# Holding raw stores and the rounding of seven late weight blocks until the first layer is nearly done

## The chip, the cores and the metric

One core of one Trainium2 chip runs the whole program. The metric is the device time of one execution in microseconds (us), the median of several runs. Other names used throughout: TensorE (PE in the profile) does the matrix products, ScalarE (ACT), VectorE (DVE) and GpSimd (POOL) the elementwise work, SyncE (SP) issues most DMA transfers. Lines of the changed kernel stand seven lines lower than the same lines of the kernel before from line 290 on (L872 there is L879 here, L881 is L888, L349 is L356).

## The reference, cut to what matters

```python
# attention, 8 batches, 8 heads, 576 tokens, 64 per head
q_s = exp(q - max(q, -1));  q_s = q_s / (sum(q_s, -1) + 1e-9)       # per token and head
k_s = exp(k - max(k, 2));   k_s = k_s / (sum(k_s, 2) + 1e-9)        # over the tokens
x = einsum(q_s, einsum(k_s, v))                                     # then (batch, token, 512)
# Fourier mixing and a feed-forward block
u  = x + real(fft(fft(x, axis=1), axis=2))
un = (u - mean(u)) / sqrt(var(u) + 1e-6)
out = u + maximum(un @ w_ch1, 0) @ w_ch2        # w_ch1 512 x 2048, w_ch2 2048 x 512
```

The two weights arrive as 64-bit floats. The kernel reads them as pairs of 32-bit words and rounds them to 32-bit floats on the chip.

## The kernel before

Group 0 (the first batch) uses the weights while they are still arriving. They come in 32 blocks of 512 KB, 0 to 15 of the first weight, 16 to 31 of the second. TensorE runs the first layer of group 0 as 16 products ("f"), then its second layer (the "down stage"). The attention and the Fourier mixing of batch 1 are woven into the down stage, and the same stage computes combinations of weight quarters, which are stored to HBM so that later groups can use a multiplication with seven products instead of eight. From the next group on nothing of this recurs.

Rounding a block takes two passes on ScalarE, two on VectorE, and one addition on GpSimd. The intermediate `t` lies in PSUM for blocks below 20, and over the block's own raw words, in SBUF, for the rest.

```python
n = ("bc", "bb", "bc", "bb")[i] if i < 4 else "acc"
if i < 20:
    t = self.ps.tile([P, 512], F32, tag=n, name=n, bufs=3 if i >= 4 else 1)[:]   # PSUM
else:
    t = hi.bitcast(F32)                                                          # SBUF
...
nc.scalar.activation(t, hi.bitcast(F32), ACT.Copy, scale=2.0 ** -112)                      # L347
V.tensor_scalar(out=to, in0=ti, scalar1=3, ..., op0=ALU.logical_shift_left)                # L348
V.scalar_tensor_tensor(out=to, in0=ti, scalar=-(1 << 31), in1=to, ...)                     # L349
nc.scalar.activation(lo, lo.bitcast(U32), ACT.Copy, scale=2.0 ** -29)                      # L352
nc.gpsimd.tensor_tensor(out=out, in0=to, in1=lo, op=ALU.add)                               # L353
```

Raw words wait in places that are used again. After a block is rounded, the next block of the same place is fetched:

```python
def round_blocks(some):
    for i in some:
        convert(i)
        if i in after:
            fetch(after[i])          # 29 takes the place of 25, 31 that of 26
...
for f in range(NF):                  # the first layer, one product and one Relu each
    up[f]()
    free(f)                          # at f 12 queries may be loaded, at 15 keys and values, quarters stored
    round_blocks(...)
rest = [lambda i=i: round_blocks([i]) for i in range(4 + n, 2 * NF)]   # 20 to 31, woven into the down stage
...
# in combine(layer, p), which stores combinations
if layer and p % 4 == 3:
    four = self.spare_words          # pairs 3 and 7: in "spare", the same memory as unT
```

The program gives each engine its order by a static schedule made at build time, so a block that stands "in the down stage" of the program may be rounded during the layer, as soon as its words are there. `unT` is the normalized, turned input of a group's first layer.

## Time and profile before

The time is 1136.21 us (3 runs, 1135.63 to 1138.32). What matters is read off TensorE's timeline, from the first product of the layer to the first product of the next group (L942). "End gap" is from the end of the last down matmul (its start in the timeline plus 0.43 us for each record) to that product, so it holds the last turns of the input too.

| stage, kernel before | us |
|---|---|
| first layer, first product to first down matmul | 66.48 (with one wait of 7.41) |
| down stage | 73.45 (with waits of 0.60 and 1.15) |
| end gap | 1.28 |
| start of the next group | 204.44 |

Two stretches of the windows view, the beginning of the down stage. The columns are the stretch, its length, then busy time (and instruction count) of TensorE, its weight loads, VectorE, ScalarE and GpSimd, TensorE's granted clock, the DMA share and GB/s:

```profile
117.20:129.70 12.50, 12.49 (x24) 5.44 (x25) 4.53 (x11) 7.48 (x23) 3.39 (x4) 0.83 0.33 109
129.70:146.00 16.30, 15.70 (x49) 7.64 (x48) 13.59 (x33) 8.20 (x24) 9.94 (x12) 1.00 0.88 321
```

### The profile page before, as it was taken

The numbers are of one execution on the slowest core, as the hardware profiler recorded it, in microseconds if no ns is written. First come the engines' busy times: TensorE is split into PE (matmuls) and PEld (weight loads), VectorE is DVE, ScalarE is ACT, GpSimd is POOL, SyncE is SP. The second block draws the span as 40 slices with busy tenths as digits, with TensorE's granted clock in tenths as the row PEclk, the third lists the DMA queues.
The fourth block names the chain that finished last, engine by engine and source line by source line (L and its number), as shares of the span: only waits on it lengthen the run. The fifth ranks groups of instructions, "written<-read, shape, count | busy, mean of one in ns | idle before, by whom it ended". The sixth has DMA issues, their size and how long they took to land.

```text
span 1134.4 us, 14587 instructions
## 1 busy us (share of the span) xinstructions
PE 1094.5 (96%) x5440; PEld 915.5 (81%) x5440; DVE 542.3 (48%) x1109; ACT 404.3 (36%) x975; POOL 335.3 (30%) x304
## 2 busy tenths in 40 slices
PE   5798899999999999999999999999999999999997
PEld 4643355888888988898889888888889888888886
DVE  6776586368433734375344733583434352203201
ACT  6694423355333513362325322442334152201200
POOL 2065382226103510334023402261034203302320
PEclk9999899999999999999999999999999999999999
DMA  9556668354346534544356335552453344434441
GB/s 304 174 200 186 231 218 303 116 206 176 111 151 220 185 142 145 194 157 176 127 176 220 149 102 179 193 200 107 144 193 148 116 156 156 182 143 156 151 186 55
DMA packets 92581, 193.79 MB, mean 171 GB/s; under 512 B 23120, under 2 KB 59728, under 8 KB 85344
## 3 DMA queue, kind: packets, MB, share of 16 engines
q1 hardware_dynamic: 90712, 191.82, 49.2%
q10 hardware_dynamic: 1800, 1.05, 0.3%
q8 instruction: 43, 0.70, 0.2%
q14 instruction: 26, 0.21, 0.1%
HBM read 168.72 MB, written 28.31 MB: 174 GB/s over the span
## 4 chain that ended last, share of the span: by engine, by line
PE 86%; ACT 4%; DMA 3%; DVE 3%; issue 2%; POOL 1%; ACTq 0%; SPq 0%; POOLq 0%; DVEq 0%
PE bb L942 15%; PE bb L980 15%; PE ba L942 10%; PE bc L980 10%; PE bc L942 10%; PE ba L980 10%; PE acc L563 3%; PE acc L645 2%; PE acc L738 2%; PE acc L741 2%; PE acc L762 2%; PE tr L613 1%; PE tr L842 1%; PE bc L881 1%; PE tr L549 1%
## 5 line engine op out<-in xcount | busy, mean ns | idle before, releaser
L942 PE MATMUL bb<-unT,big 128*128 128x256 f32 x768 | 187.4, 381 | 0.0
L980 PE MATMUL bb<-big 128*128 128x256 f32 x768 | 172.1, 379 | 0.0
L942 PEld LDWEIGHTS bb<-unT,big 128*128 128x128 f32 x768 | 142.8, 190 | 23.6 <-DVE u L910 2.6
L980 PEld LDWEIGHTS bb<-big 128*128 128x128 f32 x768 | 145.4, 190 | 20.3
L359 POOL TENSOR_TENSOR big<-big 128x512 f32<-128x512 f32 (+1 forms) x38 | 46.2, 1217 | 305.9 <-ACT big L954 305.9
L942 PE MATMUL bc<-unT,big 128*128 128x256 f32 x512 | 125.4, 379 | 0.0
L954 ACT ACTIVATE big<-big 128x512 f32<-128x512 f32 x96 | 60.3, 629 | 182.6 <-DVE big L953 182.1
L942 PE MATMUL ba<-unT,big 128*128 128x256 f32 x512 | 123.6, 379 | 0.2 <-ACT unT L846 0.2
L980 PE MATMUL bc<-big 128*128 128x256 f32 x512 | 116.0, 379 | 0.5 <-DVE x L997 0.5
L980 PE MATMUL ba<-big 128*128 128x256 f32 x512 | 114.8, 379 | 0.0
L914 DVE TENSOR_TENSOR u<-bb,s 128x512 f32<-128x512 f32 x40 | 27.6, 691 | 177.8 <-PE bb L980 120.4
L980 PEld LDWEIGHTS bc<-big 128*128 128x128 f32 x512 | 96.1, 190 | 14.3 <-DVE x L997 0.9
L980 PEld LDWEIGHTS ba<-big 128*128 128x128 f32 x512 | 95.7, 190 | 12.1
L942 PEld LDWEIGHTS bc<-unT,big 128*128 128x128 f32 x512 | 95.1, 190 | 12.6
L942 PEld LDWEIGHTS ba<-unT,big 128*128 128x128 f32 x512 | 95.1, 190 | 12.2 <-ACT unT L846 0.5
L367 POOL TENSOR_TENSOR unT<-unT 128x512 f32<-128x512 f32 x8 | 14.2, 1774 | 182.1 <-DVE unT L366 182.1
L602 ACT ACTIVATE q<-q,qm 128x64 f32<-128x64 f32 x240 | 61.6, 339 | 6.1 <-DVE qm L600 6.0
L910 DVE TENSOR_TENSOR u<-bb,s 128x512 f32<-128x512 f32 x40 | 27.6, 690 | 73.3 <-PE bb L942 38.7
L953 DVE TENSOR_TENSOR big<-bc,u 128x512 f32<-128x512 f32 x64 | 44.1, 689 | 22.8 <-PE bc L942 21.7
L992 POOL TENSOR_TENSOR x<-x,u 128x512 f32<-128x512 f32 x14 | 17.7, 1267 | 113.9 <-DVE u L914 101.3
L846 ACT COPY unT<-tr 128x512 f32<-128x512 f32 x36 | 20.7, 586 | 79.7 <-PE tr L842 79.1
L953 DVE TENSOR_TENSOR big<-bb,s 128x512 f32<-128x512 f32 x32 | 22.1, 690 | 55.6 <-PE bb L942 55.5
(248 smaller groups left out, 1653.9 us busy)
## 6 DMA issues: line engine op xcount, KB each, us to landing
big<-w1s SPq DMA_DIRECT2D x64, 896.0 KB
big<-w2s SPq DMA_DIRECT2D x56, 1024.0 KB
big<-in_w_dram SPq DMA_DIRECT2D x21, 512.0 KB
q<-in_q_dram SPq DMA_DIRECT2D x27, 256.0 KB
k<-in_kT_dram SPq DMA_DIRECT2D x24, 288.0 KB
v<-in_v_dram SPq DMA_DIRECT2D x24, 256.0 KB
words<-in_w_dram SPq DMA_DIRECT2D x8, 512.0 KB
mirror<-x SPq DMA_DIRECT2D x14, 256.0 KB
```

The costliest lines, as they stand in the source:

```text
L359: e1.tensor_tensor(out=to(4), in0=at(2), in1=at(3), op=ALU.add)
L563: nc.tensor.matmul(pk, lhsT=ks[:, c, :], rhs=v[:, c, :], start=(c == 0), stop=(c == NC - 1))
L602: nc.scalar.activation(heads[:, h, :], heads[:, h, :], ACT.Exp, bias=m[:, h:h + 1])
L645: nc.tensor.matmul(px[:, r * P:(r + 1) * P], lhsT=qT[:, r, :], rhs=self.kvr[b % 2][:, r, :], start=True, stop=True)
L738: nc.tensor.matmul(full[:, at:at + size], lhsT=t[:, own], rhs=self.ft[:, f + at:f + at + size], start=at == 0, stop=False, skip_group_chec ...
L741: nc.tensor.matmul(full[:, 0:NM], lhsT=g[:, tail], rhs=self.ft[:, f:f + NM], start=False, stop=True, skip_group_check=True)
L910: V.tensor_tensor(out=temp("u2"), in0=box["bb"][:], in1=box["s1"][:], op=ALU.add)
L914: V.tensor_tensor(out=temp("u3"), in0=box["bb"][:], in1=box["s1"][:], op=ALU.add)
L942: nc.tensor.matmul(bank()[:, i, :], lhsT=w[:, WA_AT[m], k * P:(k + 1) * P], rhs=unT[:, B_AT[m], k, :], start=first and i == 0 and k == 0, ...
L953: V.tensor_tensor(out=hp(i), in0=bank[:], in1=u[:], op=ALU.add)
L954: nc.scalar.activation(hp(i), hp(i), ACT.Relu)
L980: nc.tensor.matmul(bank()[:, i, :], lhsT=h[p][:, A_AT[m], i * P:(i + 1) * P], rhs=w[:, p, :], start=first and i == 0 and p == 0, stop=p == ...
```

## The change

Its intent is to get late roundings and the first weight's stores out of the way of the layer. A gate is a tiny VectorE instruction that reads one tile and rewrites a few words of another, so that users of the second wait for the first. Here blocks 20 to 26 wait for the Relu of product 13, and the raw quarters' stores wait for the end of the layer.

```diff
             for t in held.get(f, ()):
                 copy(t, self.h0[0:1, f, 0:1])
-            if f == NF - 1:
-                copy(self.w1sb[0:1, :, 0:1], self.w1sb[0:1, :, 0:1])
         return free
+
+    def hold_stores(self):
+        for w in (self.w1sb[0:1, :, ::HD], self.w2sb[0:1, 0:3, ::HD]):
+            self.nc.vector.tensor_copy(w, w)
+        for i in range(NF + 4, 2 * NF):
+            if i in self.raws:
+                self.gate(self.h0[:, NF - 3, :], self.raws[i][0:1, 0:2])
 ...
                 round_blocks(range(4 + n * f // NF, 4 + n * (f + 1) // NF))
+            blk.hold_stores()
             rest = ...
```

## The prediction

> **What bounds the kernel now.** I read the page first, then TensorE's timeline from 56 to 206 us, then the timelines of the other engines over the gaps found there. TensorE is busy 96% of the span, so a change is worth only what it does to TensorE's gaps (and to the clock after them). The change touches one place: the stage between the first feed-forward layer of batch 0 and the first layer of the next group. Compiled instruction orders of the two kernels, which need no chip, are the same on TensorE from end to end, and on every engine again from about 20 us into the next group. The other ~925 us can only be shifted.
>
> ```profile
> span 1134.4 us, 14587 instructions
> PE 1094.5 (96%) x5440; PEld 915.5 (81%) x5440; DVE 542.3 (48%) x1109; ACT 404.3 (36%) x975; POOL 335.3 (30%) x304
> ```
>
> TensorE's timeline (start, length, line, count of records, idle time before): the one large gap, and the end of the stage.
>
> ```profile
> 106.20 3.60 PE L872 MATMUL ba<-unT,big 128*128 128x512 f32 x8
> 117.21 5.80 PE L872 MATMUL bb<-unT,big 128*128 128x512 f32 x8 [7.41 <-ACT big L874]
> 122.84 3.60 PE L872 MATMUL bc<-unT,big 128*128 128x512 f32 x8
> 126.27 3.60 PE L872 MATMUL ba<-unT,big 128*128 128x512 f32 x8
> 129.71 3.60 PE L881 MATMUL bc<-big 128*128 128x512 f32 x8
> ...
> 202.30 1.02 PE L881 MATMUL bc<-big 128*128 128x512 f32 x2
> 203.16 1.04 PE L842 MATMUL tr<-ident,eo 128*128 128x128 f32 x8
> 204.44 1.99 PE L942 MATMUL ba<-unT,big 128*128 128x256 f32 x8 [0.24 <-ACT unT L846]
> ```
>
> Each f of the layer takes 3.43 us (start to start). Product 13 waits 7.41 us for a Relu that frees its bank, then takes 5.63 instead of 3.43. Why is that Relu late? ScalarE's timeline:
>
> ```profile
> 101.12 0.58 ACT L874 ACTIVATE big<-ba 128x512 f32<-128x512 f32 x1
> 111.53 0.65 ACT L347 ACTIVATE big<-big 128x512 f32<-128x512 f32 x1 [9.82 <-DMA big<-in_w_dram]
> 112.09 0.66 ACT L352 ACTIVATE big<-big 128x512 int32<-128x512 uint32 x1
> 115.38 0.65 ACT L347 ACTIVATE words<-words 128x512 f32<-128x512 f32 x1 [2.63 <-DMA words<-in_w_dram]
> 115.94 0.66 ACT L352 ACTIVATE words<-words 128x512 int32<-128x512 uint32 x1
> 116.49 0.57 ACT L874 ACTIVATE big<-bb 128x512 f32<-128x512 f32 x1
> ```
>
> ScalarE is not short of work time; it sits at the rounding of blocks 29 and 31, whose words were only requested at 107.98 and 110.04, and Relu 10 stands behind them. That is what the change removes. At the stage's end, unT (the normalized input of the next group) is copied from 201.25 on:
>
> ```profile
> 201.25 0.59 ACT L846 COPY unT<-tr 128x512 f32<-128x512 f32 x1
> 203.80 1.08 ACT L846 COPY unT<-tr 128x512 f32<-128x512 f32 x2 [0.71 <-PE tr L842]
> ```
>
> Its tile is the same memory as "spare", which holds raw words and, for combination pairs 3 and 7 of the second weight, four results. Before, that is over in time (GpSimd, then the queue issues the store):
>
> ```profile
> 184.60 0.73 POOL L369 TENSOR_TENSOR spare<-big,spare 128x256 f32<-128x256 f32 x1 [0.36 <-DVE spare L368]
> 189.63 1.10 SPq L402 DMA_DIRECT2D w2s<-spare x1
> ```
>
> **What the Trainium skill says.** "PSUM — Partial Sum Buffer", section "Engine vs sequencer instructions": the queues of ScalarE, VectorE and GpSimd are strict FIFO. The trace agrees: Relu 10 had its product by about 103 us and ran at 116.49, behind two roundings. "TensorE: Matmul & The Clock Gate", section "What's actually happening": after an idle window of about 3.4 us the array falls to half clock and needs about as long of busy time to come back. The trace agrees: 5.63 against 3.43 us after the gap, 2.2 us lost. "DMA: Bandwidth & Descriptors", section "Specifications": about 358 GB/s per core from HBM. From 157 to 195 us this trace moved 336 GB/s with the engines 98% busy, which I use, though single slices reached 423.
>
> **The change part by part.**
>
> *Layer one.* After the change the roundings of blocks 20 to 26 stand behind Relu 13 (a gate on VectorE reads Relu 13's output and each raw block), and the fetches of 29 and 31, which need the places of 25 and 26, come later still. Relu 8 to 13 stand directly behind one another. So product 13 starts at 106.20 + 3.43 = 109.63, 14 at 113.07, 15 at 116.50, and the down stage at 119.94 instead of 129.71: **-9.77 us** (7.41 wait, 2.2 clock, rest rounding).
>
> *What is moved into the down stage.* Seven blocks times ScalarE 2 x 0.56 = 7.8 us, VectorE 0.43 + 0.69 = 7.8 us, GpSimd 1.28 = 9.0 us; VectorE's gates cost 7 x 0.08 = 0.6. Stores: 8 of 128 KB (first weight's raw quarter), 2 of 128 and 5 of 256 KB (second weight), plus two fetches of 512 KB: 3.6 MB, at 336 GB/s 10.7 us of transfer, into a stretch whose DMA was 9% busy for 11 us (146 to 157). In bytes it fits, with nothing over.
> Call the start of the down stage D. TensorE's own order sets deadlines, read off the old timeline: first query turned at D+8.6, block 20 needed at D+10.7, query copies at D+14.3, +18.9, +22.9, +26.8, block 24 at D+25.9, block 28 at D+38.9. Walking the new orders with the durations above from q landing at about 113.4 (requested at 110.7 once Relu 12 is done, plus 2.8 as in the old trace): blocks 20 to 23 are rounded by about 126 (deadline 130.7), the first query is ready at about 126.7 (128.5), blocks 24 to 27 by 138 (145.8). The tight one is the third query copy, D+22.9 = 142.8: ahead of it on ScalarE stands block 29, fetched at about 136.5 and landing 4.2 to 5.2 us later (as 95.3 to 99.5 and 110.0 to 115.3 in the old trace), then 2 x 0.56 + two copies of 0.5: about 143.5. I allow **+1.0 us**. Against that, the old waits of 0.60 (query copy) and 1.15 us (Z copies behind two key exponentials; now one stands there, later) probably go: **-1.5 us**.
>
> *The end of the stage.* This I take to decide the case. In the new orders VectorE runs the second key's gate and maximum, and the combinations of pairs 6 and 7, **behind** the last down output (it waits for the last down matmul, old time 203.16). ScalarE's second key exponential stands before the unT copies, and the first unT copy also waits for the store w2s<-spare of pair 7. In old time, with durations from the old trace: output add 203.36 to 204.0, gate and key maximum to 204.8, exponential with its accumulator read to 205.7, reciprocal to 206.0, pair 6 on VectorE (2 x 0.43) to 206.9, pair 7 (0.43 + 0.83) to 208.2, GpSimd's last 0.73 to 209.4, store issued at 209.5 behind 0.9 MB of others, landed about 4 us later (a 512 KB store in the chain took 0.35 + 3.56) at 213.5. Then a copy 0.6, turn 0.64, copy 0.6, and the next group's first product at about 215.5 instead of 204.44: **+11.1 us**. TensorE is idle for 11 us there, so it starts cold: **+2.1 us**, the same as the old loss at 117 and 1.8 at 63.23 (5.37 against 3.60).
>
> Sum: -9.77 + 1.0 - 1.5 + 11.1 + 2.1 = +2.9 us; 1136.2 + 2.9 = 1139.1, and I take **1138.5 us** since the +1.0 may not come. The gap is moved from 110 us to the end of the down stage and hardly shrinks.
>
> **The rivals.**
> (a) The gain comes through: the unT copies do not really wait for the pair 7 store (I misread which transfer their semaphore stands for), only for the key exponential. Then the end costs 3.2 us (first copy at 205.7 instead of 201.25, third at 207.0) and perhaps 1 of clock, and the time is about 1130. For it: the gap of 7.4 us is real and goes. Against: the store reads the tile that the copy overwrites, so some wait must stand there.
> (b) The DMA queue or the in-order issue becomes the bound in the down stage: SyncE's queue issues in order, and behind a blocked store stand fetches 29 and 31 and the keys. For it: 98% busy DMA from 157 to 195 before, 3.6 MB more now. Against: 11 idle microseconds before it, and 9 idle after. It would add 3 to 6 us of waits at the query copies or at the Z copies: about 1143.
> (c) The shift is hidden: nothing, because later stages absorb it. Against: TensorE is over 99% busy from 204 on, with the same order, so a shift at 204 goes through to the end whole.
>
> **Range and chances.** (a) gives 1130, mine 1138.5, (b) 1143. I give mine two chances in three and the others most of the rest. Predicted **1138.5 us**, 8 in 10 between **1131.5** and **1144.0**. 2% is 22.7 us, which no rival reaches: faster 0.01, same 0.97, slower 0.02.
>
> **What would show it.** Right: no gap before product 13, its 8 records 3.6 us long; the down stage starts near 120; between the last L881 matmul and the first matmul of the next group about 11 us, ended by ScalarE's unT copy, and that copy waiting for DMA w2s<-spare; the next group's first matmuls slow; group start near 207 with the clock loss. Wrong: a first copy that waits only for the key exponential (rival a); TensorE waiting several microseconds on query or Z copies between 130 and 190 (rival b); stores landing much faster or slower than 4 us; pair 7 already combined before the last down matmul.

## The result, and the profile after

| | before | after |
|---|---|---|
| time, median (range, runs) | 1135.92 (1134.13 to 1138.32, 4) | 1151.45 (1148.95 to 1153.52, 4) |
| first layer | 66.48 | 56.70 |
| down stage | 73.45 | 87.87 |
| end gap | 1.28 | 12.61 |
| start of the next group | 204.44 | 218.93 |

The ratio is 1.0134, 95% interval 1.0106 to 1.0163. Ratios here and below are the mean time of one kernel's runs over that of the other's in the same rounds, so they are not quite the ratio of the medians. The change made the kernel 15 us slower; 1138.5 had been predicted, and the range ended at 1144.0.

TensorE's timeline of the changed kernel (start, length, line, record count, idle time before and its releaser):

```profile
108.15 3.60 PE L879 MATMUL bb<-unT,big 128*128 128x512 f32 x8
...
118.45 3.60 PE L888 MATMUL bc<-big 128*128 128x512 f32 x8
...
129.43 0.63 PE L620 MATMUL tr<-ident,q 128*128 128x128 f32 x4 [2.23 <-issue]
...
147.01 1.56 PE L652 MATMUL acc<-kvr,qT 128*128 128x128 f32 x8 [2.29 <-ACT qT L627]
...
174.74 0.73 PE L745 MATMUL acc<-ft,eo 128*128 128x144 f32 x4 [1.46 <-DVE eo L713]
187.42 0.71 PE L769 MATMUL acc<-cd,Z 128*128 128x128 f32 x4 [2.39 <-ACT Z L751]
...
217.14 1.97 PE L849 MATMUL tr<-ident,eo 128*128 128x128 f32 x8 [10.66 <-ACT unT L853]
```

Product 13 starts at 108.15 with no wait: the large gap of the layer is gone. The last line is the gap at the end that had been predicted. The four between were not: with one of 0.95 us at 149.52 they make 9.32 us of waits in the down stage, against 1.75 before. Three of them also cost clock: the work from 129.43 to 136.74 took 7.3 us and took 5.6 before, that of 147.01 to 155.0 took 7.0 (without the 0.95) against 3.9, that of 187.4 to 192.1 took 4.6 against 2.8, in sum 6.6 us. Waits and clock together account for the stage's 14.4 us.

The same two stretches as above, now of the changed kernel:

```profile
117.20:129.70 12.50, 10.27 (x27) 4.45 (x26) 11.81 (x20) 11.94 (x35) 11.14 (x11) 1.00 0.71 236
129.70:146.00 16.30, 15.02 (x52) 7.82 (x50) 16.30 (x26) 7.62 (x19) 12.35 (x12) 0.90 0.56 199
```

VectorE is busy 16.30 of 16.30 us in the second stretch, for fewer instructions than before (26 against 33). So the average instruction is longer (the mix is another one too). Groups of its roundings from 113 to 166 us (busy time, mean ns of one); L355 is the first of the two passes, L356 the second:

```profile
L356 DVE SCALAR_TENSOR_TENSOR big<-big 128x512 int32<-128x512 int32 x5 | 5.3, 1065 | 0.1
...
L355 DVE TENSOR_SCALAR big<-words 128x512 int32<-128x512 int32 x4 | 3.7, 932 | 0.0
...
L355 DVE TENSOR_SCALAR big<-big 128x512 int32<-128x512 int32 x5 | 2.1, 411 | 0.0
```

The working of the prediction used 0.43 us for the first pass and 0.69 for the second. Not every pass is stretched: five first passes took 0.41. Over all twelve blocks of this stretch the means are 0.70 and 1.08, over the seven late ones 0.55 and 1.18, in sum 12.1 us for the seven where 7.8 had been predicted. Where the rest comes from is seen by laying VectorE's timeline beside GpSimd's. First GpSimd, then VectorE:

```profile
116.38 1.30 POOL L360 TENSOR_TENSOR big<-big,words 128x512 int32<-128x512 int32 x1 [23.03 <-ACT big L881]
...
125.39 1.52 POOL L360 TENSOR_TENSOR big<-big 128x512 int32<-128x512 int32 x1
```

```profile
115.46 0.69 DVE L356 SCALAR_TENSOR_TENSOR big<-words,big 128x512 int32<-128x512 int32 x1
...
116.52 1.71 DVE L356 SCALAR_TENSOR_TENSOR big<-words,big 128x512 int32<-128x512 int32 x1
...
125.68 1.26 DVE L612 TENSOR_SCALAR qrec<-qrec 128x8 f32<-128x8 f32 x1
```

The pass at 115.46 had SBUF to itself: 0.69. The next began 0.14 us after an addition on GpSimd that ended at 116.38 + 1.30 = 117.68, and ended 0.55 us after that: it stood still while GpSimd ran. The third is telling: an addition of 1e-9 to 128 x 8 numbers lasts 1.26 us and ends at 126.94, just after GpSimd's addition (125.39 + 1.52 = 126.91). This is what the Trainium skill says in "SBUF — State Buffer", section "Who interferes with whom": a VectorE instruction with two SBUF inputs contends with a GpSimd instruction that reads SBUF, copies and tensor_scalar can contend too, and "the other **fully blocks** (not throttle)"; one with at most one SBUF input outside those modes does not contend. The trace agrees in each of these lines; the last part is met in run f1 below. The prediction missed this page. Added up, VectorE's instructions between 116.52 and 129.33, where the first query is ready, took 5.4 us more than the same instructions take undisturbed in this trace.

Last, ScalarE, in the down stage and at its end:

```profile
144.78 0.66 ACT L354 ACTIVATE big<-big 128x512 f32<-128x512 f32 x1 [5.82 <-DMA big<-in_w_dram]
...
216.50 1.07 ACT L853 COPY unT<-tr 128x512 f32<-128x512 f32 x2 [7.55 <-DMA w2s<-spare]
```

The first is block 29: its words were requested at 140.13 (136.5 had been predicted), and the third query copy stands behind it. The second is the predicted wait of the unT copy for pair 7's store.

Block 29's place was not what held its request. The place of block 25 was free at 134.05, when GpSimd's addition ended; but SyncE issues in order, and ahead of the fetch stood the store of a combination that VectorE finished only at 138.43. GpSimd, VectorE, then SyncE:

```profile
130.81 3.24 POOL L360 TENSOR_TENSOR big<-big 128x512 int32<-128x512 int32 x2
138.02 0.41 DVE L369 TENSOR_TENSOR s<-big,s 128x256 f32<-128x256 f32 x1
138.46 0.32 SPq L412 DMA_DIRECT2D w1s<-s  x1
140.13 0.38 SPq L335 DMA_DIRECT2D big<-in_w_dram  x1
```

### The profile page after: what moved, and what is told of

The parts are those of the page before. It is cut to its first block, busy times and chain, and to the rows that moved or that the text cites.

```text
span 1150.3 us, 14585 instructions
## 1 busy us (share of the span) xinstructions
PE 1099.4 (96%) x5440; PEld 917.4 (80%) x5440; DVE 546.8 (48%) x1117; ACT 404.4 (35%) x975; POOL 336.1 (29%) x304
## 4 chain that ended last, share of the span: by engine, by line
PE 88%; DVE 4%; DMA 2%; ACT 2%; POOL 2%; issue 1%; SPq 0%; ACTq 0%; POOLq 0%
PE bb L949 15%; PE bb L987 14%; PE ba L949 10%; PE bc L987 10%; PE bc L949 10%; PE ba L987 10%; PE acc L570 3%; PE acc L652 2%; PE ba L879 2%; PE acc L769 2%; PE acc L745 1%; PE acc L748 1%; PE tr L849 1%; PE bc L888 1%; PE bc L879 1%
## 5 line engine op out<-in xcount | busy, mean ns | idle before, releaser
L987 PEld LDWEIGHTS ba<-big 128*128 128x128 f32 x512 | 95.7, 190 | 12.1
```

What stands on the lines that cost most here:

```text
L987: nc.tensor.matmul(bank()[:, i, :], lhsT=h[p][:, A_AT[m], i * P:(i + 1) * P], rhs=w[:, p, :], start=first and i == 0 and p == 0, stop=p == ...
```

## The experiments

After the trace the theory was: the layer and the end came out as predicted; the down stage did not, because the late blocks' VectorE work is stretched by GpSimd and everything behind it, the fetch of 29 too, comes late. The rivals were the held stores (a crowd on the DMA queues), and the sheer number of late blocks. The sixteen runs below are all correct; "before" was run again beside each set (medians 1134.47 to 1135.43). The stage columns are from each profiled run, in us; "waits" is the sum of TensorE's waits above 0.3 us in the down stage. In e4 and f3 a wait of 2.74 and 0.89 us stands just before the first down matmul; it belongs to the layer column. The build makes the static order anew for every edit, and the traces show it. In e3 every engine keeps the order of the changed kernel. In f1, f2 and i1 (beside the changed kernel), e4 and i2 (beside the kernel before), i4 (beside e4), h1 and h2 (beside g1), TensorE's order is kept, but VectorE's and GpSimd's moved, and in all of these but f1 ScalarE's too. The layer began cold in the profiled runs of before, after and f1 (its first eight products took 5.37 us) and warm in the others (3.67), with the same code there; so 1.7 us in the layer column are such a difference between runs.

| run | layer | down | waits | end gap | time | ratio (95%) |
|---|---|---|---|---|---|---|
| before | 66.48 | 73.45 | 1.75 | 1.28 | 1135.9 | |
| after | 56.70 | 87.87 | 9.32 | 12.61 | 1151.5 | 1.0134 (1.0106, 1.0163) |
| e1_gates_only | 55.01 | 92.53 | 14.5 | 8.37 | 1152.0 | 1.0150 (1.0133, 1.0167) |
| e2_stores_only | 65.35 | 78.43 | 4.03 | 8.28 | 1148.4 | 1.0120 (1.0098, 1.0143) |
| e3_pair7_elsewhere | 55.01 | 85.58 | 8.87 | 4.49 | 1145.2 | 1.0097 (1.0082, 1.0112) |
| e4_gate_29_31 | 57.92 | 79.61 | 5.90 | 1.27 | 1132.8 | 0.9985 (0.997, 1.0) |
| f1_psum_stage | 56.71 | 81.93 | 7.90 | 12.60 | 1145.3 | 1.0084 (1.0069, 1.0099) |
| f2_gate_25_26 | 55.01 | 79.01 | 5.41 | 12.27 | 1143.5 | 1.0064 (1.0047, 1.008) |
| f3_gate29_early_q | 65.42 | 77.27 | 4.11 | 1.28 | 1140.1 | 1.0035 (1.002, 1.005) |
| f4_psum_pair7 | 55.01 | 80.77 | 7.31 | 4.50 | 1140.4 | 1.0043 (1.0026, 1.006) |
| g1_q_on_gpsimd | 55.44 | 82.01 | 6.68 | 1.28 | 1132.0 | 0.9977 (0.996, 0.9994) |
| g2_all_three | 55.01 | 79.04 | 4.86 | 4.49 | 1137.8 | 1.0024 (1.001, 1.0038) |
| h1_all_psum | 55.00 | 71.17 | 0 | 1.28 | 1123.1 | 0.9898 (0.9883, 0.9914) |
| h2_29_31_psum | 55.24 | 75.43 | 3.17 | 1.28 | 1126.6 | 0.9927 (0.9915, 0.994) |
| i1_after_all_psum | 55.01 | 80.52 | 6.82 | 12.62 | 1147.3 | 1.0097 (1.0076, 1.0117) |
| i2_before_all_psum | 56.47 | 72.84 | 1.29 | 1.28 | 1125.8 | 0.9914 (0.9896, 0.9932) |
| i3_psum_pair7 | 55.01 | 80.83 | 8.23 | 4.49 | 1140.3 | 1.0041 (1.0026, 1.0056) |
| i4_gate29_psum | 55.00 | 71.50 | 0 | 1.27 | 1123.4 | 0.9891 (0.9874, 0.9907) |

### The two halves of the change

The first run keeps the gates and drops the held stores; the second keeps the held stores and drops the gates.

```diff
 # e1: the changed kernel
-        for w in (self.w1sb[0:1, :, ::HD], self.w2sb[0:1, 0:3, ::HD]):
-            self.nc.vector.tensor_copy(w, w)
+        self.nc.vector.tensor_copy(self.w1sb[0:1, :, 0:1], self.w1sb[0:1, :, 0:1])
 # e2: the changed kernel
-        for i in range(NF + 4, 2 * NF):
-            if i in self.raws:
-                self.gate(self.h0[:, NF - 3, :], self.raws[i][0:1, 0:2])
```

> Only the gates on the seven late blocks; the raw stores are held as in the kernel before. In its compiled order pair 7's combination stands behind the last down output (as in the changed kernel), but both key exponentials stand ahead of the Z copies (as before). Theory E (the end of the stage costs about 13 us because pair 7's store must land before unT is copied) plus theory D (the seven roundings crowd VectorE and GpSimd in the down stage, 14 us): product 13 without a gap; down stage (first L881-type product to last down product) about 85 us against 73.4 before; gap before the next group about 9 us (no key exponential in the chain); time 1146 to 1150. Rival S (the held stores and their DMA traffic make the down stage slow, not the roundings): down stage near 74 us and time near 1137.

> Only the wider hold of the stores, no gates. The roundings of blocks 29 and 31 again stand before Relu 10, so theory D/E expects the 7 us gap before product 13 back, a down stage of 72 to 76 us, pair 7's combination behind the last down output with a gap of about 8 us before the next group and a cold clock after it: time about 1145 (1136 + 7.6 + 2). Rival S: down stage 80 us or more from the moved stores, time 1150 or more. If pair 7 does not matter: 1136.

Gates alone: 1152.0, and a down stage of 92.5. Stores alone: 1148.4, with the layer's wait back and pair 7's store still late:

```profile
116.63 5.51 PE L876 MATMUL bb<-unT,big 128*128 128x512 f32 x8 [8.11 <-ACT big L878]
...
213.76 1.97 PE L846 MATMUL tr<-ident,eo 128*128 128x128 f32 x8 [6.32 <-ACT unT L850]
```

So the held stores are not the main thing that makes the down stage long: alone they add 5.0 us to it, with a wait of 4.03 at a Z copy, where the gates alone add 19.1. Both stages came out above what had been expected (about 85, and 72 to 76); why the gates alone are worse than both together was not followed. The gates also remove the layer's wait. The gap at the end is brought by either half alone (6.4 and 6.3 us of wait for unT). The two halves do not add: each alone costs nearly as much as both.

### The end: pair 7's results elsewhere

```diff
 # e3: the changed kernel, in combine()
-            if layer and p % 4 == 3:
+            if layer and p == 3:
                 four = self.spare_words
+            if layer and p == 7:
+                four = self.w1sb[:, NP:NP + 2, :].rearrange("p a n -> p (a n)")
```

> The changed kernel, but pair 7 keeps its four results in rows 8 and 9 of the first weight (free once pair 4's store has read them) instead of in the tile that unT shares. The compiled order at the end is the same otherwise: key maximum and key exponential still stand behind the last down output. Theory E: the unT copy no longer waits for the store w2s<-spare; the gap before the next group falls from 10.7 to about 3 us, ended by the key exponential, with less loss of clock after it: 1151.5 - 7.5 = 1144, down to 1142. Rival (the unT copy waits for something else too, or the order of the engines holds it): the gap stays over 8 us, time 1149 or more.

```profile
207.79 1.14 PE L851 MATMUL tr<-ident,eo 128*128 128x128 f32 x8 [3.00 <-ACT unT L855]
```

The wait falls from 10.66 to 3.00, what is left being the key exponential, and the time by 6 us to 1145.2 (1142 to 1144 had been expected). That the end was a place in memory used twice is shown. The down stage stays long (85.6).

### The down stage: stretch or amount

```diff
 # f1: the changed kernel, in convert()
-            if i < 20:
+            if i < 27:
 # f2: the changed kernel, in hold_stores()
-        for i in range(NF + 4, 2 * NF):
+        for i in (25, 26):
```

> The changed kernel, with the seven late blocks staged in a PSUM bank (as blocks 4 to 19 are) and not over their own raw words in SBUF; the work on VectorE and GpSimd is the same in number. Theory C (the down stage is longer because VectorE's two passes over the late words are stretched by GpSimd reading the same SBUF): the second pass falls from 1.07 to about 0.69 us, the first from 0.93 to about 0.6, the first query is normalised some 3 us earlier, the down stage shrinks from 87.9 to 80-83 us and the time to 1144-1147. Rival A (the amount and order of the late work and the late fetches count, not the stretch): passes get shorter but the down stage stays within 2 us of 87.9 and the time within 1149-1153. A side effect may spoil it: the bank belongs to a ring of three that TensorE's attention products use too, so TensorE could wait for a bank (a wait on VectorE big L356 before an acc product).

> The changed kernel, but only blocks 25 and 26 (whose places 29 and 31 take) wait for Relu 13; 20 to 24 are rounded during the layer again; the stores stay held. If the number of late roundings sets the length of the down stage (theories C and A alike): layer 55-58 us, down 78-82, end gap 8-12 as before since the held stores and pair 7's store remain; time 1143-1147. If instead only the late fetches of 29 and 31 and the keys behind held stores count (rival F): down stays 86-89 and the time near 1151.

Staged in PSUM, VectorE's second pass has one SBUF input instead of two. First the groups of f1 from 113 to 166 us, then an addition on GpSimd, and a pass of VectorE within it:

```profile
L355 DVE TENSOR_SCALAR big<-acc 128x512 int32<-128x512 int32 x7 | 4.8, 680 | 0.0
L356 DVE SCALAR_TENSOR_TENSOR big<-acc,big 128x512 int32<-128x512 int32 x7 | 4.7, 667 | 0.1
```

```profile
117.54 2.56 POOL L360 TENSOR_TENSOR big<-big,words 128x512 int32<-128x512 int32 x2 [22.26 <-ACT big L881]
```

```profile
117.94 0.69 DVE L356 SCALAR_TENSOR_TENSOR big<-acc,big 128x512 int32<-128x512 int32 x1
```

The second pass takes 0.69 in the middle of GpSimd's additions. The first pass is slower than an undisturbed one in SBUF (0.68 against 0.41), and the two together cost 1.35 us where they had cost 1.73 for the same seven blocks. The wait for the first query is gone and the down stage falls from 87.9 to 81.9, the time to 1145.3. In both builds five roundings stand ahead of the first query on VectorE, so its being ready in time comes from the shorter instructions; further on, some VectorE and GpSimd instructions changed places. The stretch is therefore a cause. The 6 us are what the edit gave as built, the moved order included, and they are not the whole: 8.5 us more than before remain.

With two late blocks instead of seven (f2) the down stage is 79.0, and one wait remains, 5.41 us at the third query copy. ScalarE, in f2:

```profile
142.76 0.65 ACT L354 ACTIVATE big<-big 128x512 f32<-128x512 f32 x1 [8.95 <-DMA big<-in_w_dram]
```

It sits for 8.95 us at block 29's words, requested at 138.00 behind combination stores that SyncE issues in order, and the copy stands behind it. The place itself was free at 125.03, 13 us before. So the second cause is the late request of 29, and what delays it is the order of issue.

Both fixes at the end and in the stage were then put together, once with seven and once with two late blocks.

```diff
 # f4: e3 and f1 together. g2: f4, and the gates of f2
```

> The changed kernel with both terms taken away: late blocks staged in PSUM, and pair 7's four results in another place than the one that the normalized input takes. If the terms add: end gap about 4.5 as in the pair 7 run, down stage as in the PSUM run, time 6-7 us under the PSUM run, 1138-1140 by theory C, about 1145 by rival A.

> The changed kernel with three terms taken away at once: only 25 and 26 gated, late blocks staged in PSUM, pair 7's results elsewhere. Each alone gave 8, 6 and 6 us. The first two act on the same stage: with two late blocks the stretch is small already, and what is left there is the third query copy behind block 29 (5.4 us). So I expect layer 55, down stage 78-80, end 4.5, time 1134-1137; if the terms simply added it would be 1131.

The first comes near what was expected (1140.4, 4.9 us under f1, where 6 to 7 and at most 1140 had been written). The second is at 1137.8, 0.8 us over its range: the wait behind block 29 (4.86) stays, so the terms of the down stage overlap as thought. Mended in this way the change only comes back to where it started.

To tell the rest of the stretch from the late request, all twelve blocks from 20 on were staged in PSUM.

```diff
 # i1: the changed kernel; i3: the same, with pair 7 elsewhere
-            if i < 20:
+            if i < 32:
```

> The changed kernel with blocks 20 to 31 all staged in PSUM (20 to 26 alone gave 1145.3 and a down stage of 81.9). If the rest of the stage's excess is stretched passes of 27 to 31: down stage 74-77, time 1138-1140. If it is the late words of block 29 (third query copy): a wait of 3 us or more stays at a query copy, down stage 79-82, time 1143-1146. The end gap of 12.6 stays in both.

> The changed kernel with all twelve staged in PSUM and pair 7 elsewhere. End gap 4.5 instead of 12.6, so 6 us under the first of these four: 1132-1134 where stretch is the cause, 1138-1140 where the late words are.

```profile
139.90 0.66 ACT L359 ACTIVATE big<-big 128x512 int32<-128x512 uint32 x1 [6.24 <-DMA big<-in_w_dram]
```

The down stage hardly moves (80.5 and 80.8): ScalarE still sits 6.24 us at block 29, and TensorE waits 2.61 at the query copy, then for two roundings. Times are 1147.3 and 1140.3, where the late words were expected to give 1143 to 1146 and 1138 to 1140: the rival with the late words is right in kind, both runs a little worse. The banks are shared with the attention products, and one later rounding waits 7.39 us for a bank's earlier user on VectorE; whether that is the missing microsecond was not tried.

### A smaller gate on the kernel before

If the layer's wait comes from 29 and 31 alone, it is enough to hold these two.

```diff
 # e4: the kernel before, in round_blocks()
             if i in after:
                 fetch(after[i])
+                if after[i] in (29, 31):
+                    blk.gate(blk.h0[:, NF - 3, :], blk.raws[after[i]][0:1, 0:2])
 # f3: e4, with the queries released earlier
-        held = {12: [("q", D, 3)] * 3, ...
+        held = {10: [("q", D, 3)] * 3, ...
 # g1: e4, with the first three query loads on another queue, in q_load()
-        self.nc.sync.dma_start(q, ...)
+        (self.nc.gpsimd if self.early <= 3 else self.nc.sync).dma_start(q, ...)
```

> The kernel before, its stores and its end of stage untouched, with a gate on only the two blocks whose words come last (29 and 31): their rounding waits for Relu 13, blocks 20 to 26 are rounded as early as before. In the compiled order Relus 8 to 15 are free of them and the end of the stage is as before. Theory: the 7.4 us gap and the 2.2 us of clock after it go and nothing comes back: 1136 - 9.8 = 1126. Rival G (an early down stage only meets the query copies, the keys and the weight stores earlier than they can be ready, so the gap moves whatever is gated): waits of 5 us or more between 120 and 205 us, time 1132 to 1136.

> The kernel before with the roundings of 29 and 31 behind Relu 13 (the run that gave 0.9985), and the query loads released at Relu 10 instead of 12, so that they are issued ahead of second-weight stores. If the 2.74 us gap at the start of the down stage came from the late queries: that gap and its clock loss go, down stage 75-77 us instead of 79.6, time 1128-1130 (ratio 0.994-0.996). If the gap only moves to the query copies or Z copies: 1131-1134.

> The kernel before with 29 and 31 behind Relu 13 (the run that gave 0.9985), and the first three query loads of batch 1 issued from GpSimd's queue instead of SyncE's, where they stood behind second-weight stores and fetches. Theory: the queries land 3 to 5 us earlier, the 2.74 us gap at the start of the down stage and the cold matmuls behind it go; the Z copies still stand behind two key exponentials (2 to 3 us stay). Down stage 75-77 us, time 1128-1130, ratio about 0.995. Rival: the queries land no earlier (the transfer engines are full of stores, not the queue) and it stays at 1131-1134.

In e4 the layer's products run without a wait, but 2.74 us are lost before the first down matmul, and the down stage is 6.2 us longer, with 5.90 us of waits where there were 1.75: 0.9985, as the rival had said. At the first of these waits the last two Relus stand among the query exponentials, which wait for the queries:

```profile
117.74 1.28 ACT L602 ACT_TABLE_LOAD   x1 [5.32 <-DMA q<-in_q_dram]
```

Releasing the queries two Relus earlier (f3) was a miss: the static order then put the query work before four Relus, while SyncE issued the loads only at 112.10, after the fetches of 29 (106.19) and 31 (108.25) and five stores, and they landed at 116.9; TensorE waited 6.50 us in the layer, 1140.1. Issuing them from GpSimd's queue (g1) removed the wait at the start, but the time moved only to 1132.0 where 1128 to 1130 was expected: waits of 1.38, 1.94 and 3.36 us further on took its place. In g1, then, a wait removed at the start was met later.

### Giving VectorE room

The last sets take the cure of f1 to the kernel before.

```diff
 # i2: the kernel before; i4: e4; h1: g1 with this edit
-            if i < 20:
+            if i < 32:
 # h2: g1
+            if i < 20 or i in (29, 31):
```

> The fastest version so far (29 and 31 behind Relu 13, first queries from GpSimd's queue: 0.9977), with all of the blocks 20 to 31 staged in PSUM. If VectorE's stretched passes still cost time there: the waits of 1.38 and 1.94 us at the query copies and the folds shrink, down stage 82 to 79-80, time 1129-1130. If the ring of three banks, which the attention products share, becomes the wait: TensorE waits for VectorE's second pass before acc products, down stage 83 or more, time 1132-1135.

> The same, with only 29 and 31 staged in PSUM. One pass of each was stretched, so at most 1 to 1.5 us can come back: 1131-1132, not told apart from 0.9977.

> The kernel before with blocks 20 to 31 all staged in PSUM and nothing else. The 7.41 us gap of the layer comes from late words on ScalarE, which the staging does not touch: it stays (layer 65-67). The down stage loses its two waits of 1.75 us in sum: 71.5, so group start about 2 us earlier: 1132-1134, ratio about 0.998. If instead staging is the whole of the last run's gain: 1123-1126.

> 29 and 31 behind Relu 13, all twelve staged in PSUM, queries on SyncE's queue as before. Against the run with queries on GpSimd's queue (1123.1): if the queue of the queries matters, a wait of 2 to 3 us at the start of the down stage and its clock come back, 1126-1128; if not, 1123-1124.

Three of these four came out faster than expected. In h1 and i4 TensorE runs from the first product of the layer to the next group without one wait above 0.3 us. In i4 the queries are on the usual queue and it makes no difference (0.9891 and 0.9898): with this staging the queue does not matter. h2, with two blocks staged, already gives 0.9927.

The edit does more than change an operand's place, though, since the order moves with it. In e4 VectorE makes five passes of roundings between 117 and 137 us; in i4 it makes none there, as the query work now stands ahead of them, and on ScalarE too the query copies come ahead of roundings that they stood behind. So these runs show what the staging gives as built. How much of it is the end of the blocking and how much the new order they do not tell; a run with the staging and the old order was not made.

And i2, one number changed in the kernel before, gives 0.9914. I expected the layer's wait of 7.41 us to stay, since it was a wait for words. It fell to 0.63, and the clock loss of 2.2 us behind it went too. The kernel before, GpSimd, then VectorE, then SyncE's fetch of block 29:

```profile
96.74 2.94 POOL L353 TENSOR_TENSOR big<-big,words 128x512 int32<-128x512 int32 x2 [1.45 <-DVE big L349]
```

```profile
97.04 2.93 DVE L348 TENSOR_SCALAR big<-big 128x512 int32<-128x512 int32 x2
```

```profile
107.98 0.33 SPq L328 DMA_DIRECT2D big<-in_w_dram  x1
```

The same in i2:

```profile
97.17 2.55 POOL L353 TENSOR_TENSOR big<-big 128x512 int32<-128x512 int32 x2
```

```profile
98.50 1.29 DVE L348 TENSOR_SCALAR big<-acc 128x512 int32<-128x512 int32 x2 [1.06 <-POOL big L353]
```

```profile
103.17 0.33 SPq L328 DMA_DIRECT2D big<-in_w_dram  x1
```

Two first passes took 2.93 us beside GpSimd's additions; the next pair in i2, beside one too, takes 1.29 from PSUM. Places come free sooner, and block 29 is requested 4.8 us sooner (0.8 of it because the layer began sooner in this run). But ScalarE's order is another one as well: before, Relu 10 stood behind the roundings of both 29 and 31; in i2 it stands behind one pass of 29 only, and Relu 11 behind that of 31. ScalarE in i2, L352 for 29, Relu 10, L352 for 31, Relu 11:

```profile
106.67 0.67 ACT L352 ACTIVATE big<-big 128x512 int32<-128x512 uint32 x1 [6.09 <-DMA big<-in_w_dram]
107.24 0.57 ACT L874 ACTIVATE big<-bb 128x512 f32<-128x512 f32 x1
110.48 0.67 ACT L352 ACTIVATE words<-words 128x512 int32<-128x512 uint32 x1 [2.67 <-DMA words<-in_w_dram]
111.06 0.57 ACT L874 ACTIVATE big<-bc 128x512 f32<-128x512 f32 x1
```

Behind block 31, as before, Relu 10 would have run at 111.06 or later. So of the 9.25 us by which it comes earlier (116.49 to 107.24), an estimate from these lines is 3.8 for the new order, 4.7 for the earlier words and 0.8 for the earlier start. The stretched passes are seen on the way to the late request of 29, several engines away from where the wait showed; that they are the whole cause of the wait is not shown. i4 (1123.4, 1.1% under the kernel before and 2.4% under the changed one) is among the best versions found, with h1 level to it.

## Why the prediction was wrong

Step by step, predicted and measured (us, from the two profiled runs):

| step | predicted | measured |
|---|---|---|
| layer one | -9.77 | -9.78 (66.48 to 56.70) |
| down stage | -0.5 (+1.0 - 1.5) | +14.42 (73.45 to 87.87) |
| end gap | +11.1 | +11.33 (1.28 to 12.61) |
| clock after it | +2.1 | +1.6 (third product 5.41 after the first, 3.83 before) |
| start of the layer | 0 | -1.5 (63.23 to 61.75) |
| sum | +2.9 | +16.1 (the spans, 1134.4 and 1150.3, differ by 15.9) |

- The layer was right, in mechanism and size.
- The end was right, in mechanism and size: unT's copy waited for the store of pair 7, and e3 shows that it is this place in memory.
- The clock term was right in kind and half a microsecond too large. The start of the layer, 1.5 us earlier, is chance: over all profiled runs it lay between 61.75 and 64.88, with no edit ahead of it.
- **The step that failed is the down stage**, "allow +1.0 us" and "-1.5 us". The walk through it took VectorE's passes as 0.43 and 0.69 us, measured where GpSimd was idle. Beside GpSimd's work the seven late blocks' passes took 0.55 and 1.18 on average, and small instructions between them were stretched too. "The first query is ready at about 126.7" became 129.33 (the normalizing multiplication at 128.12 lasted 1.21), past TensorE's need of D + 8.6 = 127.1; fetch 29 "at about 136.5" became 140.13 (the new trace runs 1.5 us ahead, so the slips are 4.1 and 5.1 us). It was late in SyncE's queue, not for want of a place, which was free at 134.05. So the third query copy came 2.29 us late rather than 1.0, and the later folds and key exponentials in turn. f1 brings back 6 us of the 14.4, with its moved order; f2 and i1 show that the late words of 29 are what remains first. The split of the rest between waits that follow each other was not taken further.
- The two old waits that "probably go" came back under other names (0.95, 1.46, 2.39), and three of the waits cost clock besides, 6.6 us that the sum did not hold.
- Rival (b), waits at the query and Z copies, was right about the places. Of its two causes the in-order issue is in the trace: the fetch of 29 stood behind a store that waited for VectorE, 6.1 us long in the changed kernel and 13 us in f2. The crowd on the DMA queues is not the main cause (e1, without the held stores, is worse), though the stores alone cost the stage 5.0 us (e2). The size, 3 to 6 us, was too small. Why VectorE came to that combination so late was not followed.

## What to carry to other kernels

A duration read where the neighbour engine is idle is not the duration in a stage where both are full: before moving VectorE work beside GpSimd work, check the operands, and try one of two SBUF inputs in PSUM. An edit that lets the build order the engines anew is two changes at once: compare the orders before naming a cause. A wait for data that comes late is followed back to who freed its place and when; the cheap fix may be several engines away. Moving a gap is no gain if the engine that gets the work is 83% busy there already, as VectorE was.

## What the Trainium skill lacked or had wrong

- "SBUF — State Buffer", "Who interferes with whom": it had the rule right, and this prediction would have been better for it. It doesn't draw from it that staging an intermediate in PSUM is a cure. Here the two passes took 0.68 + 0.67 us staged so, against 0.41 + 0.69 undisturbed and 0.55 + 1.18 beside GpSimd; changing one number (i2) gave 0.9% of the whole time, with the new order.
- The same page: nothing says how small an instruction can be that pays the whole block; here one of 128 x 8 numbers, 0.17 us in the median of its 36 records, took 1.26 us.
- "TensorE: Matmul & The Clock Gate", "What's actually happening", names an idle window of about 3.4 us. Here waits of 2.23 to 2.39 us, each shorter than that, were followed by losses of 1.7 to 3.1 us of clock.
- The same page says that the window is free-running, so that cold starts vary from run to run. The runs agree and give a size: the same eight products of 512 columns took 5.37 us in three profiled runs and 3.67 in fifteen, behind the same wait of 0.95 or 0.96 us.
